# Rounding phases in PSUM with TensorE, and joining VectorE's products, in an S4 convolution with a gated MLP behind it

## The chip, the core and the metric

The kernel runs on one core of a Trainium2 chip. Its time is the device time of one execution in microseconds, the median of several runs. A core has five engines with a queue each: TensorE (PE, matrix products, which it writes to PSUM), VectorE (DVE), ScalarE (ACT), GpSimd (POOL) and SyncE (SP, which issues DMAs here). They run side by side and wait for one another by semaphores; each takes its own instructions in their order.

## The reference

One block of a conditioned network: 2048 tokens, 576 channels, 128 poles for each channel. The first half is a layer norm, a convolution along the tokens with a kernel made from the poles, and a gated residual; the second half a layer norm and a gated MLP that mixes tokens (w_sp) and channels.

```python
mod = (silu(c) @ w_mod)                       # six rows of 576: sa, ca, ga, sb, cb, gb
h = layernorm(x) * (1 + ca) + sa
x = x + ga * A(h)
h = layernorm(x) * (1 + cb) + sb
x = x + gb * B(h)

def A(u):                                     # S4 convolution
    dt = exp(log_dt); logdA = dt * (A_re + 1j * A_im); dB = dt * (B_re + 1j * B_im)
    P = exp(logdA[:, :, None] * l)            # l = 0 .. 2047
    K = einsum("dn,dnl,dn->dl", C_re + 1j * C_im, P, dB).real
    y = irfft(rfft(u, 4096) * rfft(K, 4096))[:2048] + u * Dskip

def B(x):                                     # gMLP
    z = gelu(x @ w_in); z1, z2 = z[:, :2304], layernorm(z[:, 2304:])
    return (z1 * (w_sp @ z2 + b_sp)) @ w_out
```

## The kernel before

The function ssm computes the first half, the class Mlp the second (phase_a makes z2 and phase_b the token mixing and the output). The change touches only ssm, and of it the part that makes the convolution's kernel and multiplies it onto the transformed input.

The 576 channels are taken in 36 groups of 16, and a loop over 40 ticks runs them through a pipeline written out by hand. In a tick, e_unit makes the magnitudes (an exponential of a matmul's result), three groups at a time; t_unit the phases of group tick; s_unit their cosine and sine, one tick later; p_unit the complex products, two ticks later; kg_unit the sum over the poles, three; k1_unit a first transform, four ticks later. Beside them run the units of five blocks of channels: u_load and u_unit (transform of the input), z_unit (product with the transformed kernel), v_unit (inverse), y_load and y_unit (last transform, skip and residual). Ticks 0 to 7 also hold ln_pair, which normalizes two rows of tokens, transforms them and stores them over st1o to u1_d in HBM. The poles' logarithms are computed in the start, split into three bfloat16 parts, stored to HBM (pa_d, pb_d) and read back as stationary operands lb, lc and la, block by block (poles_load; the second block's load is issued in tick 7, after ln_pair).

What the change's steps touch, with lines of the kernel before:

- t_unit: four matmuls (L455) with the selection table sel as moving operand write the phases of a group, in turns, to a PSUM tile of 128x1024. ACT adds the constant MAGIC (1.5 times 2 to the 23rd, L456), which rounds to whole turns as it is written in float32. DVE takes MAGIC and the phases away (L457), which leaves the rounded value less the phase, and makes an absolute value for the cosine (L459). s_unit's two ACT passes (L464, L465) follow.
- p_unit: five DVE passes. The magnitude et of the g part (512 elements) times cosine (L475) and times sine (L477); the p part (1024) times cosine (L476), and its two halves times sine with signs (L478, L479).
- kg_unit: 32 small matmuls in float32 (L489, which the hardware runs as 64), four at a time beside each other in the array's columns. ACT copies the 256 columns of the sum to kab (L492), and puts them in another order as it writes, so that it writes with a step of four elements. d_unit (L496) adds the skip.
- k1_unit: matmuls with kab as stationary operand (L506), and a copy on ACT (L513) or DVE (L511).
- u_unit: a matmul (L548), a copy to ue (L549), and two DMAs from GpSimd's queue that swap the halves of the partitions into us (L551, L552).
- z_unit: matmuls (L561) and two DVE passes, za = product times ue (L562), zb = product times us (L563). v_unit reads za and zb in two matmuls (L570, L571), a tick later.

A scheduling layer moves instructions of an engine past each other where nothing forbids it, except for those issued through a "tied" handle, which stay in the order written. Line 145 is that handle's, so that many instructions of the start, of the end of ssm and of the MLP have this one line in the profile; they are told apart by the names of their tiles.

Of the kernel before, what the change touches and what calls it, by code (L numbers as in the profile page):

```python
# [31 lines left out]
def consts():  # L32
# [66 lines left out]
    sel[:48, 1024:1280] = sel[64:, 1280:] = rge.reshape(48, 256)  # L99
    ones = np.zeros((128, 128))  # L100
    ones[::32] = 1.0
    f = np.float32
# [55 lines left out]
def ssm(tc, I, x1_d, consts_s, dram, mod_d, mlp):  # L158
# [5 lines left out]
    with ExitStack() as ctx:  # L164
# [22 lines left out]
        sel = tb.tile([112, 1536], BF, name="sel", bufs=1)  # L187
# [194 lines left out]
        def ln_stats(i):  # L382
            x = x4s[i]
            nm = ep.tile([128, 4], F32, name="nm")
            r = ep.tile([128, 4], F32, name="r")
            if i < 2:
                junk = ep.tile([128, 4, HC], F32, name="st1o").rearrange("p (a b) d -> p a (b d)", a=2)
                ss = ep.tile([128, 4], F32, name="ss")
# [48 lines left out]
        def e_unit(g):  # L437
            c, gi = divmod(g, 9)
            lb = lt["lb", c]
            e = et[g] = tb.tile([128, 1536], F32, name="et", bufs=5)  # L440
            pa = ps2()
            for h, (l, r) in enumerate(zip(halves(lb, gi), rows(256, 512))):
                T.matmul(pa[:, h], l, r, start=True, stop=True)
            A.activation(e[:, :1024].rearrange("p (h n) -> p h n", h=2), pa, AF.Exp)
            pb = ps1()
            T.matmul(pb, lb[:, gi], sel[:, 1024:], start=True, stop=True)
            A.activation(e[:, 1024:], pb, AF.Exp)

        def t_unit(g):
            c, gi = divmod(g, 9)  # L450
            f = tb.tile([128, 2, 512], F32, name="ft", bufs=5)
            pa = ps2()
            for k, (n, c0) in enumerate((("lc", 768), ("la", 0))):
                for h, (l, r) in enumerate(zip(halves(lt[n, c], gi), rows(c0, 256))):
                    T.matmul(pa[:, h].rearrange("p (c k j) -> p k c j", c=8, k=2)[:, k], l, r, start=True, stop=True)  # L455
            A.activation(f, pa, AF.Identity, bias=magic)  # L456
            V.scalar_tensor_tensor(f, f, MAGIC, pa, op0=ALU.subtract, op1=ALU.subtract)  # L457
            ct = tb.tile([128, 2, 512], F32, name="ft", bufs=5)
            V.tensor_single_scalar(ct.bitcast(I32), f.bitcast(I32), 0x7FFFFFFF, op=ALU.bitwise_and)  # L459
            tt[g] = (f, ct)  # L460

        def s_unit(g):
            f, ct = tt[g]
            A.activation(ct, ct, AF.Sin, bias=halfpi, scale=-TWO_PI)  # L464
            A.activation(f, f, AF.Sin, scale=-TWO_PI)  # L465

        def p_unit(g):

            f, ct = tt[g]
            e = et.pop(g)  # L470
            p = tb.tile([128, 1536], F32, name="pg")
            pr, pi = [t[:, :1024].rearrange("p (c s j) -> p c s j", c=16, s=2) for t in (p, e)]
            gr, gi = [t[:, 1024:].rearrange("p (c a) -> p c a", c=16) for t in (p, e)]
            c3, s3 = [x.rearrange("p h (c k j) -> p k (h c) j", c=8, k=2) for x in (ct, f)]
            V.tensor_tensor(gr, gi, c3[:, 1], op=ALU.mult)  # L475
            V.tensor_tensor(pr, pi, c3[:, 0, :, None, :].to_broadcast([128, 16, 2, 32]), op=ALU.mult)  # L476
            V.tensor_tensor(gi, gi, s3[:, 1], op=ALU.mult)  # L477
            V.scalar_tensor_tensor(pi[:, :, 0], s3[:, 0], -1.0, pi[:, :, 0], op0=ALU.mult, op1=ALU.mult)  # L478
            V.tensor_tensor(pi[:, :, 1], s3[:, 0], pi[:, :, 1], op=ALU.mult)  # L479
            tt[g] = (pr, pi, gr, gi)  # L480

        def kg_unit(g):
            pr, pi, gr, gi = tt.pop(g)
            pm = ps1()
            for i in range(4):
                for x_, y_, st in ((gr, pr, True), (gi, pi, False)):
                    for j in range(4):
                        c = 4 * i + j
                        T.matmul(pm[32 * j:32 * j + 32, 64 * i:64 * i + 64], x_[:, c], y_[:, c].rearrange("p s j -> p (s j)"),  # L489
                                 start=st, stop=not st, skip_group_check=True)  # L490
            kk = kab[g] = tb.tile([128, 4, 64], F32, name="kab")
            A.activation(kk.rearrange("p i (b w) -> p i w b", w=4), pm[:, :256].rearrange("p (i w b) -> p i w b", i=4, w=4), AF.Copy)  # L492

        def d_unit(g):
            kk = kab[g]
# [34 lines left out]
        def part(n, bufs=2):  # L530
            return sb.tile([128, 512], F32, name=n, bufs=bufs)

        def by(t, c):
            return t.rearrange("p (k d) -> p k d", d=CHW[c])

# [7 lines left out]

        def u_unit(c, i):
            u1 = st.pop((c, i))
            ue = part("ue", 4)
            pm = ps1()
            T.matmul(pm, fwd, u1, start=True, stop=True)  # L548
            A.activation(ue, pm, AF.Copy)  # L549
            us = part("us", 4)  # L550
            G.dma_start(us[:64], ue[64:])  # L551
            G.dma_start(us[64:], ue[:64])  # L552
            st[c, i] = (ue, us)

        def z_unit(c, i):
            ue, us = st.pop((c, i))
            w = CHW[c]
            za, zb = part("za"), part("zb")
# [3 lines left out]
            V.tensor_tensor(za, pm, ue, op=ALU.mult)  # L562
            V.tensor_tensor(zb, pm, us, op=ALU.mult)  # L563
            st[c, i] = (za, zb)

        def v_unit(c, i):
            za, zb = st.pop((c, i))
            v = part("ue", 4) if c == NC - 1 and i > 1 else part("v")
            pm = ps1()
            T.matmul(pm, inva, za, start=True, stop=False)  # L570
            T.matmul(pm, invb, zb, start=False, stop=True)  # L571
            A.activation(v, pm, AF.Copy)
            G.dma_start(v_d[c][:, kr(c, i)], by(v, c))

        def y_vload(c, q):
            bs = slice(4 * q, 4 * q + 4)
            w = CHW[c]
            rows = v_d[c].rearrange("(b h g) k d -> b h (g k) d", b=16, h=2)[bs].rearrange("b h p d -> p h b d")
            if c == NC - 1:
                t = part("ue", 4)  # L580
                st["yv", c, q] = t[:, :4 * w], t[:, 4 * w:]
                for hh in range(2):
                    S.dma_start(by(t[:, 4 * w * hh:4 * w * hh + 4 * w], c), rows[:, hh])
                return
            if c == NC - 2 and q < 2:
                vt = [part("za"), part("zb")]
            else:
                vt = [part("u1", 5)[:, :4 * w] for _ in range(2)]
            st["yv", c, q] = vt
            for hh in range(2):  # L590
                S.dma_start(by(vt[hh], c), rows[:, hh])

        def y_xload(c, q):
# [3 lines left out]
            elif c == NC - 1:  # L597
                xb = mlp.x1l[:, 4 * q - 4:4 * q]
            else:
                xb = by(part("us", 4) if c == NC - 2 or (c, q) == (2, 3) else part("xb"), c)  # L600
                S.dma_start(xb, I["x"][:, bs, chan(c)])
            st["y", c, q] = xb, bs

# [1564 lines left out]
```

## Time and profile before

| | us |
|---|---|
| median of 3 runs | 1786.69 (1786.42 to 1787.71) |
| the profiled execution | 1784.31 |
| its span, first to last instruction | 1782.5 |
| groups' loop, from the first rounding pass (L457) to the last | 52.8 to 370.2 |

Times in the profile are microseconds from the span's start. A row of stretches gives the stretch, its length, the busy time of PE, of weight loads (PEld), of DVE, ACT and POOL, then the granted clock of PE, the DMA share and the rate in GB/s. A row of groups gives line, engine, operation, written and read tiles, shapes and count, then busy time in all and the mean duration of one in ns, then the idle time just before them and what ended it. A row of the timeline gives start, duration, engine, line, operation and count, and in brackets the idle time before it and what ended that. A row of waits gives who waited for whom, the sum, how often, and the longest. Durations of neighbours on an engine overlap, so the step from start to start is what an instruction adds.

### The profile page before, as it was taken

How to read it: one execution, taken by the hardware profiler on the slowest of the kernel's cores; microseconds unless marked ns; L12 is line 12 of the kernel's file. 1: busy time of each engine (PE TensorE's matmuls, PEld its weight loads, DVE VectorE, ACT ScalarE, POOL GpSimd, SP SyncE). 2: the span in 40 equal slices, each digit the busy share in tenths (PEclk: the TensorE clock that was granted, in tenths of full speed). 3: DMA queues.
4: the chain of work that ended last, by engine and by line, in shares of the span. 5: the costliest groups of instructions: out<-in, count | busy, mean ns of one | idle time of the engine just before them, and what ended most of it. 6: DMA issues, size and time to landing. Idle time of an engine off the chain costs nothing.

```text
span 1782.5 us, 36327 instructions
## 1 busy us (share of the span) xinstructions
PE 1664.0 (93%) x15094; PEld 1239.3 (70%) x15094; DVE 1265.7 (71%) x2331; ACT 854.0 (48%) x1130; POOL 247.4 (14%) x400
## 2 busy tenths in 40 slices
PE   4487899997899999999989999999999999999999
PEld 1243455565455545777877888888888888888887
DVE  6864999966999998788899777688344478344432
ACT  5877999854477666455434444234232223122210
POOL 4311232333122211000000000000111100111100
PEclk8586999998999999999999999999999999999999
DMA  9356645579689779777665886773766572556531
GB/s 276 117 175 202 175 124 167 167 210 301 210 251 293 243 227 268 279 250 254 234 215 163 285 301 236 268 247 121 251 222 231 196 233 99 192 195 218 192 111 40
DMA packets 183380, 376.04 MB, mean 211 GB/s; under 512 B 39360, under 2 KB 103488, under 8 KB 182448
## 3 DMA queue, kind: packets, MB, share of 16 engines
q1 hardware_dynamic: 140416, 175.05, 32.2%
q0 software_dynamic: 36896, 172.01, 28.7%
q10 hardware_dynamic: 5904, 26.67, 3.7%
q8 instruction: 118, 1.93, 0.4%
q14 instruction: 46, 0.38, 0.1%
HBM read 262.93 MB, written 101.31 MB: 204 GB/s over the span
## 4 chain that ended last, share of the span: by engine, by line
PE 57%; DVE 14%; DMA 5%; issue 3%; ACT 1%; POOL 0%; SPq 0%; ACTq 0%; DVEq 0%; POOLq 0%
PE ps L145 54%; DVE bsz L145 2%; DMA zset<-set_d 2%; DMA wsst<-in_w_spT 1%; DVE zset L145 1%; DVE gt L145 1%; DVE n L145 1%; DVE rq L145 1%; DVE wsp L145 1%; PE pk L145 1%; DVE wso L145 1%; DVE raw L145 1%; DVE nt L145 1%; DMA z_d<-z 1%; PE pk L561 1%
## 5 line engine op out<-in xcount | busy, mean ns | idle before, releaser
L145 PEld LDWEIGHTS <-zset 128*128 128x128 f16 x7182 | 701.9, 98 | 93.9 <-DVE zset L145 8.8
L145 PE MATMUL ps<-wsp,zset 128*128 128x256 f16 x6048 | 667.7, 273 | 8.4 <-DVE zset L145 6.8
L145 PE MATMUL pz<-wz,nt 128*128 128x512 f16 (+1 forms) x1120 | 222.3, 358 | 10.6 <-DVE nt L145 4.5
L145 ACT ACTIVATE z<-gt 128x1024 f16<-128x1024 f32 x56 | 59.0, 1054 | 281.7 <-DVE gt L145 281.7
L145 PEld LDWEIGHTS <-nt 128*128 128x128 f16 x1120 | 108.8, 98 | 117.9 <-DVE nt L145 5.9
L145 DVE SCALAR_TENSOR_TENSOR gt<-ps,sc,bsp 128x512 f32<-128x512 f32 x36 | 27.0, 749 | 204.8 <-PE ps L145 203.0
L1876 POOL DMA_DIRECT2D zset<-set_d x96 | 51.0, 532 | 870.5 <-PE ps L145 623.2
L145 PE MATMUL ps<-wout,z 128*128 128x288 f16 x1344 | 170.0, 286 | 0.0
L145 PEld LDWEIGHTS <-z 128*128 128x128 f16 x1344 | 131.5, 98 | 33.0
L145 PE MATMUL ps<-n2o,zset 128*128 128x256 f16 x1134 | 128.2, 273 | 0.0
L145 DVE SCALAR_TENSOR_TENSOR gt<-ps,sc,gt 128x512 f32<-128x512 f32 (+1 forms) x180 | 122.2, 696 | 7.9 <-DVE gt L145 0.5
L145 DVE TENSOR_TENSOR raw<-raw 128x512 f32<-128x512 f32 (+2 forms) x228 | 119.1, 528 | 10.6 <-DMA raw<-z_d 6.3
L145 ACT ACTIVATE zset<-raw 128x1792 f16<-128x1792 f32 x48 | 81.2, 1691 | 63.2 <-PE ps L145 39.5
L145 DVE TENSOR_TENSOR zset<-raw,zset 128x1792 f16<-128x1792 f32 x48 | 97.0, 2020 | 17.4 <-ACT zset L145 16.2
L145 DVE TENSOR_TENSOR z<-ps,z 128x512 f32<-128x512 f32 (+1 forms) x126 | 72.0, 598 | 36.8 <-ACT z L145 25.1
L145 ACT ACTIVATE wsp<-raw,sc 128x1792 f16<-128x1792 f32 x25 | 44.6, 1785 | 42.9 <-DVE raw L145 35.2
L145 ACT ACTIVATE z<-z,sc 128x1024 f32<-128x1024 f32 x21 | 24.1, 1148 | 75.6 <-DVE z L145 71.9
L457 DVE SCALAR_TENSOR_TENSOR ft<-ft,ps 128x1024 f32<-128x1024 f32 x36 | 43.7, 1214 | 22.4 <-ACT ft L456 22.4
L145 ACT ACTIVATE z<-z,nm,r 128x1152 f32<-128x1152 f32 x24 | 31.4, 1342 | 51.1 <-DVE nm L145 30.5
L145 ACT ACTIVATE z<-pz,sc 128x512 f32<-128x512 f32 (+1 forms) x96 | 51.5, 584 | 8.8 <-DMA z_d<-z 4.8
L145 PE MATMUL ps<-n2q,wf 128*128 128x512 f16 x252 | 55.7, 379 | 0.0
L506 PEld LDWEIGHTS pk<-small,kab 128*64 128x64 f32 x576 | 34.2, 145 | 28.9 <-issue 17.3
(359 smaller groups left out, 2507.6 us busy)
## 6 DMA issues: line engine op xcount, KB each, us to landing
zset<-set_d POOLq DMA_DIRECT2D x96, 896.0 KB, 4.9
raw<-z_d SPq DMA_DIRECT2D x48, 512.0 KB, 5.5
set_d<-zset ACTq DMA_DIRECT2D x24, 896.0 KB, 6.0
z_d<-z POOLq DMA_DIRECT2D x32, 576.0 KB, 9.0
zset<-wa_d POOLq DMA_DIRECT2D x18, 896.0 KB, 4.9
raw<-in_w_spT SPq DMA_DIRECT2D x25, 512.0 KB, 4.8
set_d<-zset SPq DMA_DIRECT2D x12, 896.0 KB, 5.9
u_d<-st1o POOLq DMA_DIRECT2D x16, 576.0 KB, 4.0
```

The source lines that it names most:

```text
L145: return self.tc.keep_in_program_order(f(*a, **k))
L457: V.scalar_tensor_tensor(f, f, MAGIC, pa, op0=ALU.subtract, op1=ALU.subtract)
L506: T.matmul(pm[64 * ri:64 * ri + 64, 128 * i:128 * i + 128], kk[:, i], r1[ri], start=True, stop=True, skip_group_check=True)
L561: T.matmul(pm[:, w * j:w * j + w], cst[k // 8][:, k % 8], k1t[c][:, k, :w], start=True, stop=True)
L1876: self.nc.gpsimd.dma_start(o, self.set_d[f, j - 1] if j else self.wa_d[f])
```

## The change

Five edits, all in ssm and in the constants that it reads:

1. In the first ten groups, TensorE rounds the phases. t_unit issues 12 matmuls for these groups in place of four: two that write MAGIC to all 512 columns of each bank, four that add the phases, two that take MAGIC away, and four that take the phases away. VectorE then copies the result from PSUM; ScalarE has no pass. The other groups are as before.
2. p_unit writes the two products of the g part in one VectorE pass of 1024 elements. For this, cosine and sine lie in one tile (three buffers of a pair in place of five single ones), and the products in a tile of 2048 elements in place of 1536.
3. z_unit writes both products in one VectorE pass. For this, ue and us become halves of a tile uu, and za and zb halves of zz; the function half hands out single halves of uu where the end of ssm used ue and us for other things.
4. kg_unit's matmuls read their moving operand in the order in which kab is wanted (a step of 16 elements), and ScalarE's copy to kab is contiguous.
5. The table sel has 2368 columns in place of 1536. A small tile of the layer norm, ss, has one buffer.

```diff
-    sel = np.zeros((112, 1536))
+    sel = np.zeros((112, 2368))
     sel[:48, :1024] = sel[64:, :1024] = half
+    for h in range(0, 112, 64):
+        rows = slice(h, h + 48)
+        sel[rows, 1536:1792] = -half[:, 768:]
+        sel[rows, 1792:2048] = -half[:, :256]
+        sel[h, 2048:2112] = MAGIC
+        sel[rows, 2112:2240] = 1.0
+        sel[rows, 2240:] = -1.0
...
+        NR = 10
+
         def t_unit(g):
             c, gi = divmod(g, 9)
-            f = tb.tile([128, 2, 512], F32, name="ft", bufs=5)
+            cs = tb.tile([128, 2, 2, 512], F32, name="ft", bufs=3)
+            ct, f = cs[:, 0], cs[:, 1]
             pa = ps2()
...
+            def phases(cols, start, stop):
+                for k, (n, c0) in enumerate(zip(("lc", "la"), cols)):
+                    for h, (l, r) in enumerate(zip(halves(lt[n, c], gi), rows(c0, 256))):
+                        T.matmul(pa[:, h].rearrange("p (c k j) -> p k c j", c=8, k=2)[:, k], l, r, start=start, stop=stop, skip_group_check=True)
+
+            def magics(c0, start):
+                for h, (l, r) in enumerate(zip(rows(c0, 128), rows(2048, 64))):
+                    T.matmul(pa[:, h].rearrange("p (c j) -> p c j", c=8), l, r[:, None, :].to_broadcast([48, 8, 64]), start=start, stop=False,
+                             skip_group_check=True)
+
+            if g < NR:
+                magics(2112, True)
+                phases((768, 0), False, False)
+                magics(2240, False)
+                phases((1536, 1792), False, True)
+                V.tensor_copy(f, pa)
+            else:
+                phases((768, 0), True, True)
+                A.activation(f, pa, AF.Identity, bias=magic)
+                V.scalar_tensor_tensor(f, f, MAGIC, pa, op0=ALU.subtract, op1=ALU.subtract)
...
         def p_unit(g):
...
-            V.tensor_tensor(gr, gi, c3[:, 1], op=ALU.mult)
-            V.tensor_tensor(pr, pi, c3[:, 0, :, None, :].to_broadcast([128, 16, 2, 32]), op=ALU.mult)
-            V.tensor_tensor(gi, gi, s3[:, 1], op=ALU.mult)
...
+            gri = p[:, 1024:].rearrange("p (x c a) -> p x c a", x=2, c=16)
+            V.tensor_tensor(gri, e[:, None, 1024:].rearrange("p x (c a) -> p x c a", c=16).to_broadcast([128, 2, 16, 32]), cs[:, 1], op=ALU.mult)
+            V.tensor_tensor(pr, pi, c3[:, :, None, :].to_broadcast([128, 16, 2, 32]), op=ALU.mult)
...
         def kg_unit(g):
...
-                        T.matmul(pm[32 * j:32 * j + 32, 64 * i:64 * i + 64], x_[:, c], y_[:, c].rearrange("p s j -> p (s j)"),
+                        T.matmul(pm[32 * j:32 * j + 32, 64 * i:64 * i + 64], x_[:, c], y_[:, c].rearrange("p s (h t) -> p t (s h)", h=2),
...
-            A.activation(kk.rearrange("p i (b w) -> p i w b", w=4), pm[:, :256].rearrange("p (i w b) -> p i w b", i=4, w=4), AF.Copy)
+            A.activation(kk, pm[:, :256].rearrange("p (i b) -> p i b", i=4), AF.Copy)
...
+        def half():
+            if not spare:
+                uu = sb.tile([128, 2, 512], F32, name="uu", bufs=4)
+                spare.extend((uu[:, 1], uu[:, 0]))
+            return spare.pop()
...
         def z_unit(c, i):
...
-            V.tensor_tensor(za, pm, ue, op=ALU.mult)
-            V.tensor_tensor(zb, pm, us, op=ALU.mult)
-            st[c, i] = (za, zb)
+            V.tensor_tensor(zz, pm[:, None, :].to_broadcast([128, 2, 512]), uu, op=ALU.mult)
+            st[c, i] = zz
```

More of the change, by code (lines that the diff above doesn't have):

```diff
@@ L96, in consts @@
     half = np.concatenate([rgt.reshape(48, 256), rpe.reshape(48, 512), rpt.reshape(48, 256)], axis=1)
-    sel = np.zeros((112, 1536))
+    sel = np.zeros((112, 2368))
     sel[:48, :1024] = sel[64:, :1024] = half
-    sel[:48, 1024:1280] = sel[64:, 1280:] = rge.reshape(48, 256)
+    for h in range(0, 112, 64):
[5 more added lines that the diff above has]
+        sel[rows, 2240:] = -1.0
+    sel[:48, 1024:1280] = sel[64:, 1280:1536] = rge.reshape(48, 256)
     ones = np.zeros((128, 128))
@@ L186, in ssm @@
         tb = tabs.enter_context(tc.tile_pool(name="tb", reuse_waits="tile", bufs=2))
-        sel = tb.tile([112, 1536], BF, name="sel", bufs=1)
+        sel = tb.tile([112, 2368], BF, name="sel", bufs=1)
         dsk = tb.tile([128, 144], F32, name="dsk", bufs=1)
@@ L387, in ln_stats @@
                 junk = ep.tile([128, 4, HC], F32, name="st1o").rearrange("p (a b) d -> p a (b d)", a=2)
-                ss = ep.tile([128, 4], F32, name="ss")
+                ss = ep.tile([128, 4], F32, name="ss", bufs=1)
                 for b in range(4):
@@ L445, in e_unit @@
             pb = ps1()
-            T.matmul(pb, lb[:, gi], sel[:, 1024:], start=True, stop=True)
+            T.matmul(pb, lb[:, gi], sel[:, 1024:1536], start=True, stop=True)
             A.activation(e[:, 1024:], pb, AF.Exp)
+        NR = 10
         def t_unit(g):
             c, gi = divmod(g, 9)
-            f = tb.tile([128, 2, 512], F32, name="ft", bufs=5)
+            cs = tb.tile([128, 2, 2, 512], F32, name="ft", bufs=3)
+            ct, f = cs[:, 0], cs[:, 1]
             pa = ps2()
-            for k, (n, c0) in enumerate((("lc", 768), ("la", 0))):
-                for h, (l, r) in enumerate(zip(halves(lt[n, c], gi), rows(c0, 256))):
-                    T.matmul(pa[:, h].rearrange("p (c k j) -> p k c j", c=8, k=2)[:, k], l, r, start=True, stop=True)
@@ L456, in t_unit @@
-            A.activation(f, pa, AF.Identity, bias=magic)
-            V.scalar_tensor_tensor(f, f, MAGIC, pa, op0=ALU.subtract, op1=ALU.subtract)
-            ct = tb.tile([128, 2, 512], F32, name="ft", bufs=5)
+            def phases(cols, start, stop):
+                for k, (n, c0) in enumerate(zip(("lc", "la"), cols)):
+                    for h, (l, r) in enumerate(zip(halves(lt[n, c], gi), rows(c0, 256))):
+                        T.matmul(pa[:, h].rearrange("p (c k j) -> p k c j", c=8, k=2)[:, k], l, r, start=start, stop=stop, skip_group_check=True)
@@ L459, in t_unit @@
             V.tensor_single_scalar(ct.bitcast(I32), f.bitcast(I32), 0x7FFFFFFF, op=ALU.bitwise_and)
-            tt[g] = (f, ct)
+            tt[g] = cs
         def s_unit(g):
-            f, ct = tt[g]
+            ct, f = tt[g][:, 0], tt[g][:, 1]
             A.activation(ct, ct, AF.Sin, bias=halfpi, scale=-TWO_PI)
@@ L467, in p_unit @@
         def p_unit(g):
-            f, ct = tt[g]
+            cs = tt[g].rearrange("p x h (c k j) -> p k x (h c) j", c=8, k=2)
             e = et.pop(g)
-            p = tb.tile([128, 1536], F32, name="pg")
+            p = tb.tile([128, 2048], F32, name="pg")
             pr, pi = [t[:, :1024].rearrange("p (c s j) -> p c s j", c=16, s=2) for t in (p, e)]
[L473 to L476, printed above, removed]
-            V.tensor_tensor(gi, gi, s3[:, 1], op=ALU.mult)
-            V.scalar_tensor_tensor(pi[:, :, 0], s3[:, 0], -1.0, pi[:, :, 0], op0=ALU.mult, op1=ALU.mult)
-            V.tensor_tensor(pi[:, :, 1], s3[:, 0], pi[:, :, 1], op=ALU.mult)
-            tt[g] = (pr, pi, gr, gi)
+            gri = p[:, 1024:].rearrange("p (x c a) -> p x c a", x=2, c=16)
+            c3, s3 = cs[:, 0, 0], cs[:, 0, 1]
+            V.tensor_tensor(gri, e[:, None, 1024:].rearrange("p x (c a) -> p x c a", c=16).to_broadcast([128, 2, 16, 32]), cs[:, 1], op=ALU.mult)
+            V.tensor_tensor(pr, pi, c3[:, :, None, :].to_broadcast([128, 16, 2, 32]), op=ALU.mult)
+            V.scalar_tensor_tensor(pi[:, :, 0], s3, -1.0, pi[:, :, 0], op0=ALU.mult, op1=ALU.mult)
+            V.tensor_tensor(pi[:, :, 1], s3, pi[:, :, 1], op=ALU.mult)
+            tt[g] = (pr, pi, gri[:, 0], gri[:, 1])
         def kg_unit(g):
@@ L531, in part @@
             return sb.tile([128, 512], F32, name=n, bufs=bufs)
+        spare = []
+        def half():
[3 more added lines that the diff above has]
+            return spare.pop()
         def by(t, c):
@@ L545, in u_unit @@
             u1 = st.pop((c, i))
-            ue = part("ue", 4)
+            uu = sb.tile([128, 2, 512], F32, name="uu", bufs=4)
             pm = ps1()
             T.matmul(pm, fwd, u1, start=True, stop=True)
[L549 to L553, printed above, removed]
+            A.activation(uu[:, 0], pm, AF.Copy)
+            G.dma_start(uu[:64, 1], uu[64:, 0])
+            G.dma_start(uu[64:, 1], uu[:64, 0])
+            st[c, i] = uu
         def z_unit(c, i):
-            ue, us = st.pop((c, i))
+            uu = st.pop((c, i))
             w = CHW[c]
-            za, zb = part("za"), part("zb")
+            zz = sb.tile([128, 2, 512], F32, name="zz")
             pm = ps1()
@@ L561, in z_unit @@
                 T.matmul(pm[:, w * j:w * j + w], cst[k // 8][:, k % 8], k1t[c][:, k, :w], start=True, stop=True)
-            V.tensor_tensor(za, pm, ue, op=ALU.mult)
-            V.tensor_tensor(zb, pm, us, op=ALU.mult)
-            st[c, i] = (za, zb)
+            V.tensor_tensor(zz, pm[:, None, :].to_broadcast([128, 2, 512]), uu, op=ALU.mult)
+            st[c, i] = zz
         def v_unit(c, i):
-            za, zb = st.pop((c, i))
-            v = part("ue", 4) if c == NC - 1 and i > 1 else part("v")
+            zz = st.pop((c, i))
+            v = half() if c == NC - 1 and i > 1 else part("v")
             pm = ps1()
-            T.matmul(pm, inva, za, start=True, stop=False)
-            T.matmul(pm, invb, zb, start=False, stop=True)
+            T.matmul(pm, inva, zz[:, 0], start=True, stop=False)
+            T.matmul(pm, invb, zz[:, 1], start=False, stop=True)
             A.activation(v, pm, AF.Copy)
@@ L579, in y_vload @@
             if c == NC - 1:
-                t = part("ue", 4)
+                t = half()
                 st["yv", c, q] = t[:, :4 * w], t[:, 4 * w:]
@@ L585, in y_vload @@
             if c == NC - 2 and q < 2:
-                vt = [part("za"), part("zb")]
+                zz = sb.tile([128, 2, 512], F32, name="zz")
+                vt = [zz[:, 0], zz[:, 1]]
             else:
@@ L599, in y_xload @@
             else:
-                xb = by(part("us", 4) if c == NC - 2 or (c, q) == (2, 3) else part("xb"), c)
+                xb = by(half() if c == NC - 2 or (c, q) == (2, 3) else part("xb"), c)
                 S.dma_start(xb, I["x"][:, bs, chan(c)])
```

## The prediction

> **What bounds the kernel now.** I read the page first, for its totals, then the busy time by stretches of the span, because the change touches only the first stage (the convolution's kernel, its transform and products, up to some 410 us).
>
> ```profile
> span 1782.5 us, 36327 instructions
> PE 1664.0 (93%) x15094; PEld 1239.3 (70%) x15094; DVE 1265.7 (71%) x2331; ACT 854.0 (48%) x1130; POOL 247.4 (14%) x400
> ```
>
> Over the whole span TensorE (PE) leads with 93%, which says little of the first stage. The stretches, with their length first and then busy microseconds of each engine:
>
> ```profile
> 52.00:107.00 55.00, 34.81 (x505) 17.83 (x502) 46.52 (x112) 47.14 (x67) 18.24 (x27) 0.62 0.48 148
> 107.00:157.00 50.00, 40.68 (x551) 21.88 (x547) 31.78 (x68) 37.91 (x51) 8.41 (x12) 0.73 0.48 164
> 157.00:165.00 8.00, 0.57 (x2) 0.14 (x2) 4.09 (x6) 3.38 (x3) 3.07 (x6) 0.57 1.03 284
> 191.00:345.00 154.00, 143.90 (x2097) 85.45 (x2093) 142.84 (x216) 144.49 (x187) 47.45 (x78) 0.99 0.51 146
> 345.00:398.00 53.00, 51.28 (x673) 31.81 (x671) 40.89 (x64) 34.46 (x48) 18.66 (x32) 1.00 0.78 207
> 52.00:68.00 16.00, 5.24 (x56) 1.93 (x52) 13.82 (x36) 15.88 (x26) 1.55 (x2) 0.50 0.11 40
> 135.50:147.50 12.00, 11.33 (x142) 5.72 (x138) 5.86 (x10) 11.96 (x16) 1.69 (x3) 0.50 0.39 143
> ```
>
> The columns after the length are PE, weight loads, VectorE (DVE), ScalarE (ACT), GpSimd, PE's granted clock, DMA share and GB/s. Four parts follow. Early (52 to 157 us), no engine is full, but ACT is in places (15.88 of 16 and 11.96 of 12 us), and PE runs at a clock of 0.62 to 0.73. From 157 to 165 all wait for a DMA. In the middle (191 to 345) PE, DVE and ACT are each busy some 143 of 154 us: three engines at 93 to 94%, none with room. Late (345 to 398) PE alone is full. So a saving on DVE or ACT counts early and, up to PE's own work, in the middle; nothing counts late but PE.
>
> The wait at 157 us decides how much of an early gain goes through:
>
> ```profile
> 154.72 0.75 POOL L429 DMA_DIRECT2D u_d<-st1o  x1 [1.43 <-ACT st1o L428]
> 156.83 1.26 POOL L145 DMA_DIRECT2D lb<-pb_d  x2 [0.29 <-POOL lb L145]
> PE pk L446 <- DMA lb<-pb_d: 8.4, 1, 8.4
> ```
>
> The load of the second channel block's exponents (lb), which group 9 needs, stands on GpSimd's queue behind the last store of the normalized rows (st1o), and that store waited for ACT. When ACT gets there sooner, the load, its 8.4 us of waiting and all behind them move forward together.
>
> **The change part by part.** Rounding by PE (groups 0 to 9). ACT loses one pass, and DVE's pass over PSUM becomes a copy.
>
> ```profile
> L456 ACT ACTIVATE ft<-ps,consts_s 128x1024 f32<-128x1024 f32 x36 | 40.6, 1128 | 1.9 <-PE ps L455 1.6 <-ACT et L447 0.4
> L457 DVE SCALAR_TENSOR_TENSOR ft<-ft,ps 128x1024 f32<-128x1024 f32 x36 | 43.7, 1214 | 22.4 <-ACT ft L456 22.4
> L511 DVE COPY k<-pk 128x512 f32<-128x512 f32 x13 | 8.9, 683 | 4.3 <-PE pk L506 4.3
> 192.45 0.61 PE L443 MATMUL ps<-sel,lb 48*128 48x512 bf16 x4 [0.53 <-DVE ft L457]
> 192.99 0.39 PE L446 MATMUL pk<-sel,lb 112*128 112x512 bf16 x1
> 178.55 0.28 PE L455 MATMUL ps<-sel,lc 48*128 48x256 bf16 x2
> 178.67 0.27 PE L455 MATMUL ps<-sel,la 48*128 48x256 bf16 x2
> ```
>
> ACT: 10 passes of 1.13 us leave, 11.3 us of busy time. DVE: the copy of 1024 from PSUM should cost what the old pass did (the 512 copy takes 683 ns, as other 512 passes do, so 1024 goes with 1214): nothing. PE: each group gets two pairs of 512 columns and two of 256. Two 512 pairs took 0.54 us from 192.45 to 192.99, a 256 pair 0.12 us (178.55 to 178.67): 0.54 + 0.24 = 0.78 us, at half clock up to 1.56, so 8 to 16 us in ten groups. PE is idle 20.2 us in 52 to 107 and 9.3 us in 107 to 157, which covers most of it; from 135.5 to 147.5 only 0.67 us is idle, and two groups falling there could lay some 2.4 us on the path. What counts of ACT's 11.3 us is what falls where ACT is the full engine: I take four of the nine groups ahead of the wait at 157 us, rounded down to 4.0 us; bounds are 9 x 1.13 = 10.2 us gained and 2.4 us lost.
>
> The joined products (p_unit and z_unit) each turn two DVE passes of 512 into one of 1024.
>
> ```profile
> 262.17 0.68 DVE L562 TENSOR_TENSOR za<-pk,ue 128x512 f32<-128x512 f32 x1
> 262.77 0.67 DVE L563 TENSOR_TENSOR zb<-pk,us 128x512 f32<-128x512 f32 x1
> 267.02 0.68 DVE L475 TENSOR_TENSOR pg<-et,ft 128x512 f32<-128x512 f32 x1
> 267.62 1.22 DVE L476 TENSOR_TENSOR pg<-et,ft 128x1024 f32<-128x1024 f32 x1
> 268.75 0.16 DVE L496 TENSOR_TENSOR kab<-kab,dsk 128x4 f32<-128x4 f32 x1
> 191.18 1.21 DVE L457 SCALAR_TENSOR_TENSOR ft<-ft,ps 128x1024 f32<-128x1024 f32 x1
> 344.83 1.21 DVE L457 SCALAR_TENSOR_TENSOR ft<-ft,ps 128x1024 f32<-128x1024 f32 x1
> ```
>
> The durations overlap, so I count from start to start: 0.60 us for a 512 pass (262.17 to 262.77, 267.02 to 267.62) and 1.13 for 1024 (267.62 to 268.75). One join saves 1.20 - 1.13 = 0.07 us; by durations (2 x 0.68 - 1.21) it would be 0.15. From the group at 191.18 to that at 344.83 there are 20 steps, with two joins each: 20 x 0.14 = 2.8 us. Late, PE's work covers the saving: zero. The joined z product waits for both swapping DMAs, where the first of the old two did not:
>
> ```profile
> DVE zb L563 <- DMA us<-ue: 1.3, 3, 1.0
> ```
>
> DVE had waited 1.3 us in all for them. Behind the new wait stand the rest of p_unit and the next group's rounding pass on DVE, but the second old pass made them wait just as long; the inverse matmuls, which need the product, come a step later. I take zero (at most one more pass of 0.6 us, three times).
>
> The kernel matrix's copy (kab) now writes contiguously, and the matmuls before it read their moving operand with a stride instead.
>
> ```profile
> L444 ACT ACTIVATE et<-ps 128x1024 f32<-128x1024 f32 x36 | 37.0, 1034 | 8.3 <-PE ps L443 5.3 <-PE ps L145 2.9
> L447 ACT ACTIVATE et<-pk 128x512 f32<-128x512 f32 x36 | 22.1, 613 | 4.2 <-PE pk L446 4.2
> L492 ACT ACTIVATE kab<-pk 128x256 f32<-128x256 f32 x36 | 23.3, 648 | 6.5 <-PE pk L489 6.5
> DVE ft L457 <- ACT ft L456: 7.4, 5, 2.4
> ```
>
> Two contiguous passes give (1034 - 613) / 512 = 0.82 ns an element and 192 ns fixed. At 256 elements that is 402 ns; kab took 648, so 1.78 ns an element with its 16-byte step, 2.2 times as much. ACT saves 0.25 us a group. The last row is from the middle alone: DVE waited there 7.4 us for ACT's rounding pass, five times. The relief can shorten these waits; I take 1.5 us of the 7.4. Floor for the whole middle: PE's 143.90 busy us, so no more than 10.1 us.
>
> PE's strided read of those matmuls (L489) is the operation that no row shows. I take it as free, since the same number of columns streams; its bound is in the rivals.
>
> The larger table of selections, and buffers:
>
> ```profile
> 5.93 0.70 SPq L645 DMA_DIRECT2D sel<-in_c_sel  x1
> PE ps L145 <- DMA small<-in_c_small: 9.3, 1, 9.3
> 0.00:50.00 50.00, 20.52 (x97) 7.44 (x98) 33.16 (x104) 28.68 (x61) 18.15 (x33) 0.85 0.89 256
> ```
>
> sel grows by 112 x 832 x 2 bytes = 186 KB. At 256 GB/s, with DMA 0.89 busy, it delays what is queued behind it on SP (two modulation loads, the constants, the pole loads) by 0.7 us; PE waits for those constants, so I count all of it. The three double buffers for phases free a pair after the same p_unit as before, and the halves of the joined buffers turn over in the same order: zero. After the first stage the order on every engine is the old one, so what is won or lost there shifts the end one for one.
>
> Sum: -4.0 - 2.8 - 1.5 + 0.7 = -7.6 us. The profiled execution took 1784.31 us (1.8 beyond its span), so 1776.7 on its scale; the median of the runs, 1786.69, lies 2.4 higher, and on that scale the forecast is 1779.1 us. Its own range: both ACT and DVE gains at their bounds give 10.2 + 10.1 - 0.7 = 19.6 us less, hardly to be had together; half of it again beyond my sum, 1770, and nothing gained, 1787.
>
> **The rivals.**
>
> PE pays for the stride (slower). The only strided access priced by a row is kab's write, at 2.2 times. For the matmuls:
>
> ```profile
> 262.80 0.32 PE L489 MATMUL pk<-pg 128*32 128x64 f32 x8
> 263.83 1.13 PE L548 MATMUL pk<-u,small 128*128 128x512 f32 x2
> 345.00:398.00 53.00, 6.61 (x384) 5.64 (x384) 1.00 0.78 207
> ```
>
> A group's 64 take 1.03 us (262.80 to 263.83). At 2.2 times it is +1.2 us a group. Middle: 20 x 1.2 = 24 us against PE's 10.1 idle: +13.9. Late: the last row, of L489 alone, holds 384 matmuls, six groups: 7.2 us against 1.7 idle: +5.5. With the early gain and the table, +19.4 - 4.0 + 0.7 = +16 us: 1802.8. It decides from about +0.6 us a group on: there the middle costs 12 - 10.1, the late part 3.6 - 1.7, and 3.8 us eats the early gain. For it: each element now lies 64 bytes from the last, a wider step than kab's. Against: kab is a write by another engine, and L511 reads PSUM with a step of 128 bytes at the same 683 ns as contiguous passes.
> [...]
>
> Nothing passes (no change). The DMA-bound start of the middle and PE's 143.90 us hold the pace, so only the early part moves, by 0 to 4 us: 1783 to 1787. For it: PE's summed work leaves 0.5 us a step. Against: DVE's passes stand back to back in the rows above, and its waits there end on ACT.
>
> A warmer PE (faster still). In 135.5 to 147.5 PE is busy 11.33 of 12 us at a clock of 0.50. If the added matmuls brought the full clock there, 11.33 would shrink to 5.7, and up to 5.6 us more would go: 1773.5. For it: PE is nearly full in that window. Against: ACT is fuller (11.96), and even at 11.33 of 12 the clock stayed down.
> [...]
>
> **How the numbers follow.** Chances: forecast 0.42, the stride's price 0.36, nothing passes 0.15, warmer PE 0.07. About 0.2% (3.6 us) is what a measurement of this kernel can tell from no change. Faster: nearly all of the forecast's 0.42 (its smallest gains, 0.05, fall within 0.2%) and the warm 0.07: 0.44. Same: 0.15 and that 0.05, less the part of the flat case that reaches below 1783.1: 0.18. Slower: the stride's 0.36, plus 0.02 for a lost early part: 0.38. The likeliest case's own range is 1770 to 1787; as cases of both signs hold the chance, the range runs from 1771 to 1804, which takes in the full stride price and leaves out a price beyond 2.2 times and the largest gains.
>
> **What would show it.** Right: no ACT pass for groups 0 to 9, the lb load issued near 153 us, kab at 400 ns, the joined passes at 1.21 us, L489 still 1.03 us a group, groups 12 to 32 in under 151 us. Wrong: L489 at 1.6 us or more a group and PE without idle time in the middle (the stride); the lb load at 157 or later (early part lost to PE or DMA).

## The result, and the profile after

The changed kernel takes 1798.41 us (median of four runs, 1797.78 to 1800.01) where the kernel before takes 1786.56: a ratio of 1.0072, 95% interval 1.0054 to 1.009. It is slower, by 12 us between the medians and 13 by the ratio (which is of the means); faster was forecast.

The profile of the changed kernel, page first: the span is 13.5 us longer, and TensorE has 32 us more busy time.

```profile
span 1796.0 us, 36375 instructions
PE 1696.3 (94%) x15174; PEld 1266.3 (71%) x15174; DVE 1261.3 (70%) x2259; ACT 835.5 (47%) x1118; POOL 244.9 (14%) x400
```

The same stretches as before (columns as in the prediction), and the last stretch for the pole sum's matmuls (now L513) alone:

```profile
107.00:157.00 50.00, 43.03 (x617) 23.07 (x613) 31.78 (x64) 32.83 (x47) 8.95 (x13) 0.83 0.52 171
191.00:345.00 154.00, 149.76 (x1965) 93.95 (x1965) 130.57 (x161) 131.47 (x172) 41.48 (x72) 1.00 0.46 133
345.00:398.00 53.00, 51.48 (x654) 33.83 (x652) 41.96 (x53) 36.05 (x50) 16.67 (x29) 1.00 0.68 185
345.00:398.00 53.00, 11.75 (x377) 10.39 (x381) 1.00 0.68 185
```

In the middle PE went from 143.90 to 149.76 of 154 us, and VectorE and ScalarE, level with it before, fell to 131. Most of that fall is the slower pace: fewer groups pass in the same 154 us (18.6 steps in place of 20.1, by the marks below). Late, the pole sum takes 11.75 us of PE in place of 6.61, for 377 matmuls in place of 384. The groups of instructions say which line it is; first after, then before:

```profile
L513 PE MATMUL pk<-pg 128*32 128x64 f32 x1152 | 65.9, 293 | 2.3 <-DVE vh L845 2.2
L513 PE MATMUL pk<-et,pg 128*32 128x64 f32 x1152 | 65.8, 293 | 0.9 <-DVE et L503 0.9
L500 DVE TENSOR_TENSOR pg<-et,ft 128x1024 f32<-128x1024 f32 x36 | 44.0, 1221 | 8.2 <-PE pk L513 6.6 <-ACT ft L490 1.5
L593 DVE TENSOR_TENSOR zz<-pk,uu 128x1024 f32<-128x1024 f32 x32 | 39.1, 1223 | 15.9 <-PE pk L601 7.2 <-PE pk L592 5.7 <-DMA uu<-uu 3.0
L516 ACT ACTIVATE kab<-pk 128x256 f32<-128x256 f32 x36 | 13.7, 381 | 19.3 <-PE pk L513 19.1
L479 DVE COPY ft<-ps 128x1024 f32<-128x1024 f32 x10 | 12.2, 1219 | 12.7 <-PE ps L467 12.7
```

```profile
L489 PE MATMUL pk<-pg 128*32 128x64 f32 x1152 | 42.4, 234 | 1.3 <-DVE pg L476 1.3
L489 PE MATMUL pk<-et 128*32 128x64 f32 x1152 | 41.8, 232 | 1.3 <-DVE et L479 1.3
L492 ACT ACTIVATE kab<-pk 128x256 f32<-128x256 f32 x36 | 23.3, 648 | 6.5 <-PE pk L489 6.5
```

The joined passes, the copy from PSUM and kab's contiguous write (381 ns, with 402 forecast) cost about what was forecast; a matmul of the pole sum costs 293 ns in place of 233. As these lie four beside each other in the array and overlap, a group's price is read from starts in the timeline of the changed kernel:

```profile
265.02 0.41 PE L513 MATMUL pk<-pg 128*32 128x64 f32 x8
265.24 0.44 PE L513 MATMUL pk<-et,pg 128*32 128x64 f32 x8
...
266.99 1.13 PE L580 MATMUL pk<-u,small 128*128 128x512 f32 x2
```

From the first of a group to the next line it is 1.97 us; before it was 1.03: +0.94 us a group. The pace of the groups is read from the absolute value's pass of groups 12 and 32 (before, then after):

```profile
192.99 0.68 DVE L459 TENSOR_SCALAR ft<-ft 128x1024 int32<-128x1024 int32 x1
346.64 0.68 DVE L459 TENSOR_SCALAR ft<-ft 128x1024 int32<-128x1024 int32 x1
```

```profile
187.93 0.68 DVE L484 TENSOR_SCALAR ft<-ft 128x1024 int32<-128x1024 int32 x1
353.97 0.70 DVE L484 TENSOR_SCALAR ft<-ft 128x1024 int32<-128x1024 int32 x1
```

Twenty steps took 153.65 us before and 166.04 after: 7.68 and 8.30 us a step. The change reaches group 12 five us earlier and group 32 seven us later.

### The profile page after: what moved, and what is told of

It reads as the page before. It is cut to its first block, busy times and chain, and to the rows that moved or that the text cites. A ratio compares the mean times of both kernels' runs of the same rounds, so it can differ in the third digit from the quotient of the medians.

```text
span 1796.0 us, 36375 instructions
## 1 busy us (share of the span) xinstructions
PE 1696.3 (94%) x15174; PEld 1266.3 (71%) x15174; DVE 1261.3 (70%) x2259; ACT 835.5 (47%) x1118; POOL 244.9 (14%) x400
## 5 line engine op out<-in xcount | busy, mean ns | idle before, releaser
L152 ACT ACTIVATE zset<-raw 128x1792 f16<-128x1792 f32 x48 | 81.1, 1692 | 57.5 <-PE ps L152 25.0
L513 PE MATMUL pk<-pg 128*32 128x64 f32 x1152 | 65.9, 293 | 2.3 <-DVE vh L845 2.2
L513 PE MATMUL pk<-et,pg 128*32 128x64 f32 x1152 | 65.8, 293 | 0.9 <-DVE et L503 0.9
L152 ACT ACTIVATE z<-z,sc 128x1024 f32<-128x1024 f32 x21 | 24.1, 1149 | 75.6 <-DVE z L152 71.9
```

Of the source, the lines that this page charges most:

```text
L152: return self.tc.keep_in_program_order(f(*a, **k))
```

## The experiments

The theory: TensorE pays for reading its moving operand one element at a time with a step of 64 bytes, and its added work holds the middle. The rivals: the rounding's added matmuls or the larger table cost the time, or the joined passes make something late. The table has every kernel's marks, each row from a single profiled execution, in us from the span's start: the absolute value's pass of groups 0, 10, 12, 32 and 35, the issue of the second block's lb load, and the MLP's first matmul (pz, not read for x7). The ratio is of the times, against the kernel before on the same chip.

| kernel | g0 | lb | g10 | g12 | g32 | g35 | pz | span | ratio, 95% interval |
|---|---|---|---|---|---|---|---|---|---|
| before | 54.4 | 156.8 | 178.0 | 193.0 | 346.6 | 371.9 | 453.7 | 1782.5 | |
| after | 58.3 | 156.9 | 175.7 | 187.9 | 354.0 | 381.0 | 466.9 | 1796.0 | 1.0072 [1.0054, 1.009] |
| x1 plain read | 57.4 | 155.7 | 178.1 | 190.3 | 343.5 | 367.9 | 452.8 | 1780.6 | 0.9998 [0.9983, 1.0013] |
| x2 strided read | 54.5 | 152.6 | 173.9 | 187.9 | 353.3 | 381.9 | 465.0 | 1795.4 | 1.0093 [1.0076, 1.0109] |
| x3 no rounding | 56.2 | 153.3 | 173.1 | 187.9 | 352.5 | 379.4 | 466.1 | 1796.8 | 1.0093 [1.0075, 1.011] |
| x4 joins, plain read | 56.1 | 154.9 | 176.2 | 191.7 | 345.0 | 369.3 | 452.5 | 1784.2 | 1.0002 [0.999, 1.0014] |
| x5 large table | 57.6 | 159.7 | 179.7 | 194.1 | 346.9 | 372.2 | 455.2 | 1785.0 | 1.0006 [0.9995, 1.0018] |
| x6 runs of 2 | 56.0 | 155.3 | 173.6 | 185.9 | 339.3 | 363.7 | 448.1 | 1776.9 | 0.9991 [0.9978, 1.0003] |
| x7 runs of 4 | 57.5 | 156.4 | 178.6 | 190.8 | 344.0 | 368.4 | – | 1781.8 | 1.0000 [0.9988, 1.0013] |
| x8 rounding | 56.1 | 157.2 | 176.1 | 189.7 | 341.5 | 366.8 | 449.9 | 1776.2 | 0.9977 [0.9962, 0.9992] |
| x10 rounding, plain copy | 55.6 | 157.8 | 177.0 | 190.1 | 342.1 | 367.4 | 450.4 | 1777.4 | 0.9987 [0.9976, 0.9997] |
| x11 half sum | 54.5 | 155.0 | 177.8 | 194.5 | 343.3 | 365.7 | 449.0 | 1780.0 | 0.9981 [0.997, 0.9992] |
| x12 rounding 20 | 56.6 | 156.4 | 178.2 | 193.0 | 352.0 | 377.3 | 460.4 | 1788.9 | 1.0023 [1.001, 1.0036] |
| x13 half sum, joins | 55.1 | 152.4 | 175.1 | 190.6 | 340.2 | 363.3 | 446.3 | 1776.1 | 0.9953 [0.9936, 0.997] |

**The strided read, taken out and put in alone.** x1 is the changed kernel with the old order of the matmuls; ScalarE puts kab in its order as it reads PSUM, and still writes contiguously.

```diff
-    y_[:, c].rearrange("p s (h t) -> p t (s h)", h=2)
+    y_[:, c].rearrange("p s j -> p (s j)")
-    A.activation(kk, pm[:, :256].rearrange("p (i b) -> p i b", i=4), AF.Copy)
+    A.activation(kk.rearrange("p i (b w) -> p i b w", w=4),
+                 pm[:, :256].rearrange("p (i w b) -> p i b w", i=4, w=4), AF.Copy)
```

> The changed kernel with one edit undone: the pole-sum matmuls read their moving operand in the old, contiguous order, and ScalarE reads PSUM in the permuted order instead, writing kab contiguously as the changed kernel does. Theory S (TensorE pays for the strided read): a group's 64 matmuls go back from 1.97 to about 1.03 us, kab stays near 0.38 us, and the time falls by 0.94 us in some 25 groups less the idle time that TensorE gets back, 12 to 20 us: 1778 to 1786 us. Rival R (the rounding matmuls and the larger table are what costs): the matmuls may shrink, but the time stays above 1795 us. If ScalarE pays for the permuted PSUM read, kab goes back toward 0.65 us.

x2 is the kernel before with edit 4 alone (the strided read and the contiguous write of kab).

> The kernel before with only the strided read of the pole-sum matmuls and the contiguous kab copy. Theory S: 1.97 us a group in place of 1.03; in the middle 20 x 0.94 = 18.8 us against 10.1 us of idle TensorE time, late 5.6 against 1.7: 10 to 17 us slower than before, 1797 to 1804 us. Rival R: within 4 us of before.

Without the stride the loss is gone (0.9998); with it alone the loss is all there (1.0093, some 16.6 us by the ratio). The groups of x1:

```profile
L513 PE MATMUL pk<-pg 128*32 128x64 f32 x1152 | 43.0, 237 | 2.5 <-DVE vh L845 2.4
L516 ACT ACTIVATE kab<-pk 128x256 f32<-128x256 f32 x36 | 14.0, 389 | 7.9 <-PE pk L513 7.9
```

The groups and the middle stretch of x2:

```profile
L489 PE MATMUL pk<-et 128*32 128x64 f32 x1152 | 67.2, 293 | 0.9 <-DVE et L479 0.9
L489 PE MATMUL pk<-pg 128*32 128x64 f32 x1152 | 66.1, 293 | 1.9 <-DVE pg L476 1.9
191.00:345.00 154.00, 149.19 (x1968) 94.03 (x1969) 132.94 (x199) 131.55 (x172) 41.47 (x72) 1.00 0.45 133
```

For TensorE they are the changed kernel's numbers, without its rounding and its joins. x2 also writes kab contiguously, but so does x1, without the loss. So the loss is shown to be the strided read's.

**How long a run it takes.** x6 and x7 are the changed kernel with moving operands read in runs of two and of four elements, at the same step of 64 bytes from run to run; ScalarE does the rest of the order as it reads PSUM.

```diff
-    y_[:, c].rearrange("p s (h t) -> p t (s h)", h=2)
+    y_[:, c].rearrange("p s (h t u) -> p t (s h) u", h=2, u=2)     # x7: u=4
-    A.activation(kk, pm[:, :256].rearrange("p (i b) -> p i b", i=4), AF.Copy)
+    A.activation(kk.rearrange("p i (t u w) -> p (i t) u w", u=2, w=4),
+                 pm[:, :256].rearrange("p (q w u) -> p q u w", u=2, w=4), AF.Copy)     # x7: u=4, twice
```

> The changed kernel with the moving operand of the pole-sum matmuls read in runs of two neighbouring elements (8 bytes), the rest of the order being made by ScalarE as it reads PSUM. [...] If every jump costs the same: half of the extra, about 1.5 us a group, and 1787 to 1793 us. If any order but the contiguous one costs: 1.97 us a group and 1796 us or more.

> The same with runs of four elements (16 bytes). [...] By the jump: a quarter of the extra, about 1.26 us a group, 1783 to 1790 us. By any order but the contiguous one: 1.97 us and 1796 us or more.

x6 takes 0.9991 of the time before, x7 1.0000 [0.9988, 1.0013]. The groups and one group's timeline in x6:

```profile
L513 PE MATMUL pk<-pg 128*32 128x64 f32 x1152 | 42.6, 232 | 4.0 <-DVE vh L845 3.8
L516 ACT ACTIVATE kab<-pk 128x256 f32<-128x256 f32 x36 | 14.0, 388 | 7.4 <-PE pk L513 7.3
264.74 0.32 PE L513 MATMUL pk<-pg 128*32 128x64 f32 x8
264.88 0.29 PE L513 MATMUL pk<-et,pg 128*32 128x64 f32 x8
...
265.79 1.12 PE L580 MATMUL pk<-u,small 128*128 128x512 f32 x2
```

A group takes 1.05 us: runs of 8 bytes cost nothing that can be told, single elements of 4 bytes cost 0.94 us. So neither the same price for every jump (about 1.5 us) nor one for any order but the contiguous (1.97 us) holds in x6. In x7 the matmuls take 236 and 233 ns in the mean, where x1 has 237 and 233. The step was 64 bytes in all of them; a narrower one was not run, and why two neighbours are enough is not shown.

**The parts without the stride.** x4 is the kernel before with the joined passes (edits 2 and 3), the one buffer of ss, and kab as in x1; x5 has the larger table alone, unused; x8 the rounding (with that table) alone; x10 the rounding, and kab as in x1.

> The kernel before with both joins and the contiguous kab copy, with the plain read, without rounding by TensorE and its table. My prediction's terms: 2.8 us from the joins and 1.5 us from kab, 1781 us. Rival (TensorE holds the middle, and the joins delay the end of the stage): no faster than before, or up to 4 us slower, with the step in the middle still 7.65 us.

> The kernel before with the selection table of 2368 columns loaded but its new columns unused. If the late start of the changed kernel (its third modulation product at 43.65 us in place of 39.84) is the table's: 2 to 4 us slower and the same late start. If it is chance between executions: 0.7 us, not to be told from before, and a start near 40 us.

> The kernel before with only the rounding by TensorE in the first ten groups (and its table). Theory S says that this part is not the cause: 4 us of ScalarE relief against 0.7 to 3.8 us of later start, 1783 to 1787 us. Rival R: 8 us or more slower than before.

> The kernel before with the rounding by TensorE, and with kab copied contiguously by a permuted read of PSUM; no joins, no strided read. If ScalarE's relief adds to the rounding's 0.23%: 1776 to 1780 us. If TensorE holds the middle: the same as the rounding alone, 1781 to 1783 us.

The joins and kab's relief together give nothing that can be told from zero (1.0002; the 4.3 us forecast for them would be 0.9976, outside the interval), and the table costs nothing that can be told (1.0006). The rounding alone is faster, by 0.23%. It has the lowest ratio of the versions that compute the whole result, though its interval overlaps those of x6 and x10. Relieving kab's write on top of it adds nothing that can be told (x10, 0.9987). With the joins on top as well, and no price for the stride (x1, x6, x7), the rounding's gain is not seen either; whether the joins take it back is open, as these intervals overlap too.

x3 is the changed kernel without rounding, its table small again (`NR = 0`).

> The changed kernel without TensorE's rounding and with the small table: joined passes and the strided read are left. If the stride costs its 12 us in the middle and some 4 late whatever VectorE and ScalarE do: 1799 to 1803 us, that is the changed kernel's time or up to 4 us more, by what the rounding gave. If the rounding's matmuls were a part of the loss (its late start, its larger table): 1795 us or less.

Measured: 1801.0 us and 1.0093, as x2. The stride costs the same with the joins as without them. The difference to the changed kernel's 1.0072 has the size of what the rounding gives alone (0.23%), but lies within the intervals.

**What holds the middle.** x11 is the kernel before with half of the pole sum's matmuls, x13 is x4 with the same half; x12 is x8 with the rounding in twenty groups.

```diff
-                for x_, y_, st in ((gr, pr, True), (gi, pi, False)):    # x11, x13
+                for x_, y_, st in ((gr, pr, True),):
...
-                                 start=st, stop=not st, skip_group_check=True)
+                                 start=True, stop=True, skip_group_check=True)
-        NR = 10                                                          # x12
+        NR = 20
```

> The kernel before, with the second half of the pole sum (sines' product, 32 of 64 matmuls of a group) left out; nothing else is changed, so the sum is incomplete. TensorE's own work holds the middle: each step gets shorter by up to the 0.51 us that the 32 matmuls took, until another engine's work (about 7.2 us a step) holds it, so groups 12 to 32 take 144 to 147 us in place of 153.7, the late groups gain about 0.5 us each, and the whole is 8 to 14 us faster. Rival, ScalarE or VectorE hold the middle and TensorE only waits for them: groups 12 to 32 stay at 152 to 154 us, and the whole gains under 4 us (the late groups alone).

> The kernel before with TensorE's rounding alone, in the first 20 groups in place of 10, so that eight groups of the middle have it too. TensorE holds the middle: each of these steps is longer by the 0.78 us of the added matmuls, 6 us or so, less the slack that remains; 1786 to 1790 us where the version with ten groups had 1781.9. Rival, ScalarE and VectorE hold it: each of these steps loses some of ScalarE's 1.13 us, and the whole is 2 to 7 us faster than with ten groups.

> Joined passes and the contiguous write of kab (both with a plain read by TensorE), and the second half of the pole sum left out, so that the sum is incomplete and all three engines have less to do. Three engines hold the middle together: joins alone left groups 12 to 32 at 153.3 us (153.7 before), half the sum alone brought 148.8; if VectorE and ScalarE were what held that last figure, relieving them too brings 143 to 147 us. Rival, something else (a DMA, the fixed order of the ticks) holds it: 148 to 150 us as with half the sum alone, or TensorE alone: also 148 to 150.

x11 brought groups 12 to 32 to 148.8 us, above the 144 to 147 that TensorE's theory gave and below the rival's 152, and the whole gained 3.4 us (0.9981), under the 8 to 14 that TensorE's theory gave and within the rival's 4: of 6.3 us ahead at group 35 the marks keep 4.7 at pz and 2.5 at the end. x13 had 149.65, as its rival had it; its whole gain (0.9953) is larger than x11's, and by the marks it is there before group 12, which comes 3.9 us earlier than in x11. Neither theory fits the stretch as a whole; cut at group 20 it is clearer. Before:

```profile
193.00:252.50 59.50, 55.55 (x814) 32.57 (x813) 55.15 (x85) 57.54 (x76) 18.83 (x32) 1.00 0.39 111
252.50:346.60 94.10, 88.49 (x1290) 53.32 (x1289) 87.30 (x132) 86.09 (x110) 29.17 (x48) 0.98 0.59 169
```

After:

```profile
188.00:253.30 65.30, 63.66 (x828) 39.61 (x824) 55.97 (x71) 57.62 (x78) 17.44 (x32) 1.00 0.39 111
253.30:354.00 100.70, 97.84 (x1287) 62.15 (x1288) 85.91 (x108) 84.85 (x111) 28.02 (x48) 1.00 0.55 157
```

x11, then x13:

```profile
194.50:254.00 59.50, 53.04 (x553) 29.03 (x553) 55.71 (x84) 57.68 (x76) 16.35 (x29) 0.97 0.35 101
254.00:343.30 89.30, 82.56 (x906) 46.84 (x905) 87.00 (x132) 85.51 (x111) 28.00 (x48) 1.00 0.62 179
```

```profile
190.50:251.70 61.20, 54.93 (x553) 30.29 (x553) 55.00 (x69) 56.86 (x77) 16.81 (x30) 0.94 0.34 101
251.70:340.20 88.50, 82.19 (x906) 46.60 (x906) 84.82 (x108) 83.35 (x111) 28.28 (x48) 1.00 0.62 178
```

I read these so, and it is a reading from one execution of each kernel: I take an engine at 97% to hold its stretch. (x5, which does the work of the kernel before, has 60.3 and 92.5 us in these two stretches where before has 59.5 and 94.2, so differences under some 2 us say nothing.) Before, ScalarE is there in the first (57.54 of 59.50), and half the sum doesn't shorten it (59.5 again); PE is the fullest in the second (94%), and half the sum shortens that by 4.8 us until VectorE is at 97% (87.00 of 89.30). After, PE is at 97% in both. x13 has no engine over 96%: with three engines relieved, what holds its 149.65 us is not shown; that the fixed order of the ticks does is only a guess.

x12 took 63.9 us from group 12 to 20 where x8 took 59.4: 4.6 us more for eight groups, of the 6 us expected. But TensorE is not full there. Its stretch, and its waits in that stretch:

```profile
193.00:257.00 64.00, 58.32 (x840) 33.10 (x839) 55.50 (x84) 50.71 (x68) 16.57 (x29) 1.00 0.35 98
DVE ft L477 <- PE ps L465: 6.6, 2, 3.3
ACT ft L488 <- DVE ft L483: 4.5, 4, 1.3
```

PE is at 91%, ScalarE at 79%. VectorE's copy waits for the twelve matmuls of its group (6.6 us in two waits); ScalarE's sines wait for VectorE (4.5 us in four). The size was near what TensorE's theory gave, but no engine is full as either theory had it. The waits point to a longer chain from TensorE to VectorE to ScalarE; no run tests that alone.

## Why the prediction was wrong

**The step that failed** is "PE's strided read of those matmuls (L489) ... I take it as free, since the same number of columns streams". It costs 0.94 us a group (1.03 to 1.97). The rival "PE pays for the stride" was right: its 2.2 times is 1.9, its point of decision, 0.6 us a group, was passed, and its 1802.8 us stands against 1798.4. What the prediction named as the sign of it came: over 1.6 us a group, and TensorE nearly without idle time. Its total came close in part by luck, as two of its errors met. In the middle it had 24 us of work less 10.1 us of idle time, +13.9. From group 12 to 32 PE's busy time rose by 17.5 us (55.55 + 88.49 to 63.66 + 97.84), its idle time fell by 5.1 (9.6 to 4.5), and the stretch grew by 12.4: less work was added than the rival had, and only half of the idle time was used up. Late it had +5.5; from group 32 to the MLP's first matmul it is +5.9, but x1, without the stride, already has +2.2 there (x2, with the stride alone: +4.7). The nearest row was in the prediction: kab's write with a step of 16 bytes, at 2.2 times its contiguous price. The argument from the count of columns had no row behind it at all, and it was given the sum.

The stride is not all that failed. x1 is the case that the sum describes, every edit with a free reordering, and it has 0.9998 [0.9983, 1.0013] where a gain of 7.6 us would be 0.9957.

**The joins (-2.8) and kab's relief (-1.5)** were priced about right by the pass, and gave nothing that can be told (x4: 1.0002). The rival "nothing passes" holds for them: VectorE's busy time in the middle fell from 142.84 to 139.74 us in x4, and groups 12 to 32 from 153.65 to 153.27. TensorE's 10.1 us of idle time in the middle was taken as room that the others' savings could use; it was not, and at 94% TensorE is nearly as full as any engine gets in the middle (97%). The joined z product's wait for both swapping DMAs, taken as zero beyond the old 1.3 us, is 3.0 us in the changed kernel's row of L593 above; whether it lies on the path is not shown.

**The early part (-4.0)**, with the table's +0.7, was to give 3.3 us; the rounding alone (x8) gives 0.23%, some 4 us. That is about the right size, but by luck, for it does not come where it was placed. It was to bring the lb load from 156.8 to near 153; it stands at 156.90, behind a start that is 3.8 us later. What ScalarE no longer did in groups 0 to 9 became waiting, from 58 to 157 us; before, then after (who waits for whom, sum, times, longest):

```profile
DVE pg L475 <- ACT ft L464: 14.6, 5, 5.9
```

```profile
ACT ft L489 <- DVE ft L484: 11.9, 4, 5.3
DVE pg L501 <- ACT ft L489: 8.1, 3, 5.9
```

ScalarE's sines now wait for VectorE's copy and absolute value. From group 0's pass to the lb load it is 98.7 us, as in x2 (98.1) and x3 (97.1), which have no rounding; before it was 102.4, in x8 101.0 and in x10 102.2. Of the nine kernels that write kab contiguously eight have 97.1 to 99.3 us, and the five others 99.8 to 102.4. So this part seems to go with kab's contiguous write rather than with the rounding; but x10, which has both, doesn't have it, and it is not settled. What goes with the rounding alone comes after the load: from group 9's pass to group 10's it is 2.9 to 3.9 us in all seven kernels that round by TensorE (2.92 after), and 5.3 to 6.7 in the seven that don't (6.21 before).

**The table (+0.7)** was about right where it was placed, on TensorE's wait for the constants; first before, then x5:

```profile
PE ps L145 <- DMA small<-in_c_small: 9.3, 1, 9.3
PE ps L152 <- DMA small<-in_c_small: 10.0, 1, 10.0
```

The first matmul with these constants starts at 24.1 to 25.3 us in the eight kernels with the large table and at 23.4 to 24.3 in the six with the small one, 0.9 us apart in the mean. Group 0 was late by more than that: 3.8 us after and 3.2 in x5. The rest arises behind the constants, where TensorE waits for further loads of the modulation's weights (k) and gets past them at 40.7 us after and 40.1 in x5, in place of 36.9. That part is not the table's alone: x8, with the same table, has group 0 1.7 us late, as x4 has with the small one (1.6). In the whole time of x5 the table can't be told from nothing.

**A warmer PE** was not a separate gain: in 52 to 107 us the granted clock was 0.94 after and 1.00 in x8, but 0.64 in x10 and 0.62 in x12, with the same rounding matmuls; what sets the clock is not shown. In the window that the prediction named (135.5 to 147.5 us) the clock did rise, from 0.50 to 0.73, and PE's busy time fell from 11.33 to 9.41 us, but ScalarE stayed busy for 11.69 of the 12 us.

By the marks the 13.5 us of the span are: start +3.8, from there to group 12 -8.9, groups 12 to 32 +12.4, to group 35 +1.7, to the MLP's first matmul +4.2, the rest +0.3. The last part before the MLP scatters between 81.8 us (before) and 86.7 (x3), and is 83.0 in x5, where nothing of it was changed; x1, without the stride, has 84.9, and x2, with the stride alone, 83.2. How much of its +4.2 is the stride is open.

## What to carry to other kernels

A strided operand is a cost to be priced (here 0.94 us for a group's 64 matmuls), not an order that comes for nothing: make the reordering where it is free (here in the copy that reads PSUM, 389 ns in x1 and 381 after), or keep two neighbours together (here 1.05 us a group in x6, 1.97 after). Where several engines stand level, expect little from work taken from one of them (here nothing for the joins and kab's relief, and in the middle 4.8 us for half of the pole sum, which had taken some 10 us of TensorE there), and expect most of the work added to one to go through (12.4 of 17.5 us). And if one term of the sum has no row at all, the nearest row, even from another engine, was here a better price than an argument.

## What the runs showed of the hardware

- A float32 moving operand read element by element with a step of 64 bytes made 64 matmuls, four beside each other in the array, take 1.97 us in place of 1.03 (after and x2 against before); in runs of two elements they took 1.05 (x6).
- ScalarE read PSUM with a step of 64 bytes at the price of a contiguous read (389 ns in x1, 381 after), while writing SBUF with a step of 16 bytes took 648 ns (before).
- The clock granted to TensorE in the early stage differed between kernels with the same matmuls there (0.62 to 1.00), and in these two no time followed it: x8 with 1.00 and x10 with 0.64 reached group 12 at 189.7 and 190.1 us.
